# Attention in chunks with a mixture of experts behind it: x's transposes placed ahead of the expert's blocks, and the weight steps spread otherwise

## The chip, the cores and the metric

The kernel runs on one core of one Trainium2 chip, in one launch. The time is what the device takes for one execution, in microseconds. Each number of the trace comes from one profiled execution; the time before is the median of three others.

The engines: TensorE (PE; PEld is its weight load) multiplies matrices, VectorE (DVE), ScalarE (ACT) and GpSimd (POOL) do elementwise work, and SyncE (SP) issues most DMAs. Each engine takes its instructions in the order in which the program gives them.

## The reference, cut to what matters

Attention with a decaying state, over 4 batches, 8 heads, 768 positions and head dimension 48, then eight experts (3072 tokens, width 384, hidden width 1024) under a gate that is normalised eight times over both axes:

```python
def _attn_ref(r, k, v, w, u):
    for t in range(S):
        kt, vt, rt = (k[:, :, t], v[:, :, t], r[:, :, t])
        cur = np.einsum('bhd,bhe->bhde', u[None] * kt, vt)
        y[:, :, t] = np.einsum('bhd,bhde->bhe', rt, state + cur)
        state = w[None, :, :, None] * state + np.einsum('bhd,bhe->bhde', kt, vt)
    return y

def _moe_ref(x, w_gate, w1, w2):
    logits = x @ w_gate
    logits = logits - logits.max()
    P = np.exp(logits)
    for _ in range(8):
        P /= P.sum(1, keepdims=True) + 1e-09
        P /= P.sum(0, keepdims=True) + 1e-09
        P *= N / E
    for e in range(E):
        h = np.maximum(x @ w1[e], 0.0)
        ye = h @ w2[e]
        out += P[:, e:e + 1] * ye
    return out
```

The attention's output, with heads and head dimension joined, is x of the experts.

## The kernel before, in words

Attention runs in 24 chunks of 128 positions (`NTT` = 24, six for each batch). Inside a chunk the decay is folded into the operands: r is multiplied by a table `rtab`, k by `ktab` (which follow from w and are made once, at the start, by a scan, a reciprocal and some transposes), so that scores and state are plain matrix products. The large products of the experts are made in three parts from halves in 16 bit: each operand is split into a high half and the low rest.

One loop, lines 756 to 811, runs 27 rounds, i = 0 to 26 (this text counts rounds by i, so that round 4 is the fifth). In a round three chunks are in work at different stages. In the order of the code:

- `prep(i+2)` (L493): `rp` = r times `rtab` on GpSimd, `kp` = k times `ktab` on VectorE. `bonus_dot(i+1)` (L499): two products into `rk` on GpSimd. `stage_b(i+1)` (L518): the transposes of rp and kp on TensorE, and their copies rT and kT by ScalarE.
- `scale_x(i-2)` (L606): ScalarE scales x by a power of two into `xsc`.
- `work(1)` (L729): one block of expert 0. Up to round 4, where none is ready, `spin(3)` stands in its place, three matmuls on zeros into a tile of the PSUM pool `ps2`.
- `bonus(i)` (L508): VectorE sums `rk` to `dg`, and GpSimd makes two products from it, written over `rk`; a piece of `hbx` is the second input of the last. `stage_c(i)` (L529): the scores `pA`, which VectorE copies under a mask into `at`, then `pu`, which is added to the state `S` on VectorE and scaled on GpSimd.
- `work(1)` up to round 8, `work(2)` in rounds 9 to 24 (L781 and 782).
- `stage_e(i-2)` (L612): three transposes of `xsc` into `px`, a tile of `ps2`; ScalarE casts it to the high half of x (the CAST to `hbx`), VectorE subtracts this from `px` to get the low half (`hbx<-px,hbx`). In rounds 25 and 26 `work(2)` stands behind it.
- `prepare` (L725), as often as the first number of the round in `STEPS`: one step from the list `side`.
- `stage_d(i-1)` (L573): `py`, then x = py + bonus on VectorE, its maximum `xm`, the scale (`inv_s`, `xs`).
- `prepare`, as often as the second number, then `stage_f(i-3)` (L620): six gate matmuls into `px` from `wgp` and x of this round (a tile of x has its halves in `hbx`), and the logits (`lparts`) on VectorE.

The first 24 steps of `side` split expert 0's two weights, for each of them: three maxima (`wm`) over 1024 columns, the maximum over all partitions, the scale, then high halves (ScalarE, `ws<-ws,sw`) and low halves (VectorE, `ws<-ws,sw,ws`). Behind them come steps that rebuild x of three groups of tokens and make the sums of their quarters (17 sums on GpSimd for each group, `ws<-ws` on 256 columns, after three rebuilds on VectorE); a group's steps wait in the list until its tiles have been emitted.

A block is one of two units. `g1_unit` (L214): nine matmuls into `ph`, in the pool `ps1` (2 buffers), followed by a ScalarE activation to `hb` (high half) and a VectorE operation on `ph` and `hb` (low half). `g2_half` (L236), the half of a second product: 12 matmuls into `po`, which ScalarE copies to `stg` and a DMA takes to HBM. `po` has two buffers, which it shares with `px` and the tile of `spin`. Units that the loop leaves over run behind it, one for each step of the gate's normalisation (from L988). There are 64 first-product units and 48 halves of second products. The table and the places of the blocks are these:

```python
    STEPS = {
        0: (2, 2), 1: (0, 2), 2: (3, 1), 3: (1, 1),
        4: (1, 1), 5: (1, 1), 6: (2, 2), 7: (1, 1), 8: (1, 1),
    }
```

All operations are recorded by a helper, so that L29 is the line of nearly every row.

Of the kernel before, what the change touches and what calls it, by code (L numbers as in the profile page):

```python
# [32 lines left out]
def rwkv_sinkhorn_moe(  # L33
# [13 lines left out]
    V, S_, G, T, Q = (  # L47
        InOrder(tc, e) for e in (nc.vector, nc.scalar, nc.gpsimd, nc.tensor, nc.sync)
    )
# [8 lines left out]
    NTT = NT // P  # L58
# [5 lines left out]
    HP = 64  # L64
# [193 lines left out]
    def whole(gen):  # L258
        for _ in gen:
            pass  # L260

    def merged(g1, g2):
        for n in range(max(len(g1), len(g2))):
            yield from g1[n : n + 1]
            yield from g2[n : n + 1]
# [20 lines left out]
    def spin(n):  # L286
        pz = ps2.tile([P, TB], F32, tag="po", name="pz")
        for _ in range(n):
            T.matmul(pz, zeros[:, :P], zeros, start=True, stop=True)
# [13 lines left out]
    def load_chunk(tt):  # L303
        for nm, src in (("r", r), ("k", k), ("v", v)):
            load_part(tt, nm, src)
# [36 lines left out]
    def fill(x_):  # L342
        n = x_.shape[1]
        S_.mul(
            x_.rearrange("p (a q) -> p a q", q=HP),
            unit[:, :1, 1:].broadcast_to([P, n // HP, HP]), 0.0,
        )
# [16 lines left out]
    at_ = [ac.tile([P, H, C], F32, name=f"at{i}") for i in range(2)]  # L364

    ss_ = [ac.tile([P, NPAIR, 2, D], F32, name=f"S{i}") for i in range(3)]
    for t_ in rp_ + kp_:
        G.memset(t_[:, :, D:], 0.0)
    for t_ in ss_:
        for j in range(2):  # L370
            G.memset(t_[j * HP : (j + 1) * HP, :, 1 - j, :], 0.0)
    fill(at_[0].rearrange("p h c -> p (h c)"))

    rk0 = at2.tile([P, H, D], F32, tag="rk", name="rk_0", bufs=3)
    G.tensor_tensor(rk0, loads[0]["r"], loads[0]["k"], op=ALU.mult)
# [99 lines left out]
    def gate_max():  # L475
        V.tensor_reduce(wgm, wg, axis=AX.XY, op=ALU.max, apply_absolute_value=True)

    def gate_across():
        res = over_partitions(wgm, 1, ps1, "ph", "wg")
        next(res)  # L480
        return res

    def gate_split(res):
        pow2_scale(next(res), iswg, swg, 0.25)
        S_.activation(wgh, wg, AF.Copy, scale=swg)
        V.scalar_tensor_tensor(wgl, wg, swg, wgh, op0=ALU.mult, op1=ALU.subtract)
# [6 lines left out]
    def prep(tt):  # L493
        ld_ = loads[tt]
        G.tensor_tensor(rp_[tt % 2][:, :, :D], ld_["r"], rt4, op=ALU.mult)
        V.tensor_tensor(kp_[tt % 3][:, :, :D], ld_["k"], kt4, op=ALU.mult)
        st[tt] = {}

    def bonus_dot(tt):  # L499
        ld_ = loads[tt]  # L500
        rk = rk0
        if tt:
            rk = at2.tile([P, H, D], F32, tag="rk", name=f"rk_{tt}", bufs=3)
            G.tensor_tensor(rk, ld_["r"], ld_["k"], op=ALU.mult)
        G.tensor_tensor(rk, rk, ub, op=ALU.mult)
        st[tt]["rk"] = rk

    def bonus(tt):  # L508
        vn = loads[tt]["v"]
        dg = at2.tile([P, H], F32, tag="dg", name=f"dg_{tt}")  # L510
        V.tensor_reduce(dg, st[tt]["rk"], axis=AX.X, op=ALU.add)
        av = st[tt].pop("rk")
        G.tensor_tensor(av, vn, dg.unsqueeze(2).broadcast_to([P, H, D]), op=ALU.mult)
        aq = av.rearrange("p h d -> p (h d)").rearrange("p (a q) -> p a q", q=P // 2)
        G.tensor_tensor(aq, aq, xadd(tt), op=ALU.add)
        st[tt]["av"] = av

    def stage_b(tt):  # L518
        d = st[tt]
        for nm, src in (("rT", rp_[tt % 2]), ("kT", kp_[tt % 3])):  # L520
            pt = ps3.tile([P, NPAIR, P], F32, tag="pa", name=f"p{nm}_{tt}")
            sv = src.rearrange("p (a j) d -> p a (j d)", j=2)
            for p_ in range(NPAIR):
                T.transpose(pt[:, p_, :], sv[:, p_, :], ident)
            dst = at2.tile([P, NPAIR, P], F32, tag=nm, name=f"{nm}_{tt}", bufs=3 if nm == "rT" else 2)
            S_.copy(dst, pt)
            d[nm] = dst
# [78 lines left out]
    def scale_x(tt):  # L606
        d = st[tt]
        xs = at2.tile([P, DM], F32, tag="xsc", name=f"xsc_{tt}")
        S_.activation(xs, d["x"], AF.Copy, scale=d["s"])
        d["x"] = xs  # L610

    def stage_e(tt, bank_):  # L612
        d = st[tt]
        pt = bank_[:, :DM].rearrange("p (c q) -> p c q", q=P)
        for c in range(KC):
            T.transpose(pt[:, c, :], d["x"][:, c * P : (c + 1) * P], ident)
        S_.copy(xall(tt, 0), pt)
        V.tensor_tensor(xall(tt, 1), pt, xall(tt, 0), op=ALU.subtract)

    def stage_f(tt, bank_):  # L620
        pg = bank_[:, DM : DM + 2 * E]
        for c in range(KC):
            xh_, xl_ = xall(tt, 0)[:, c, :], xall(tt, 1)[:, c, :]

            T.matmul(
                pg, xh_, wgp[:, c].rearrange("p l e -> p (l e)"), start=(c == 0), stop=False,
                skip_group_check=True,
            )
            T.matmul(
                pg[:, :E], xl_, wgh[:, c, :], start=False, stop=(c == KC - 1), skip_group_check=True  # L630
            )
        V.tensor_scalar(
            lparts[:, tt].rearrange("p l e -> p (l e)"), pg, inv_s[:, tt : tt + 1], iswg,
            op0=ALU.mult, op1=ALU.mult,
        )
        del st[tt]
# [88 lines left out]
    def prepare():  # L725
        if side and need.get(id(side[0]), 0) <= emitted[0]:
            side.pop(0)()

    def work(n, ready=True):  # L729
        if not ready:  # L730
            spin(3)
            return
        for _ in range(n):
            if units:
                whole(units.pop(0))
# [3 lines left out]
    for sg in range(3):  # L739
# [3 lines left out]

    STEPS = {
        0: (2, 2), 1: (0, 2), 2: (3, 1), 3: (1, 1),
        4: (1, 1), 5: (1, 1), 6: (2, 2), 7: (1, 1), 8: (1, 1),
    }

    def n_steps(i):
        return STEPS.get(i, (2, 2) if i < 22 else (3, 2))  # L750

    prep(0)
    prep(1)
# [2 lines left out]
    for i in range(NTT + 3):  # L756
        if i == 1:
            gate_max()
        if i + 2 < NTT:
            if i + 4 < NTT:  # L760
                load_chunk(i + 4)
            if i == 0:
                Q.dma_start(raws[1], w2[0].rearrange("(c p) d -> p c d", p=P))
            prep(i + 2)
        if i + 1 < NTT:
            bonus_dot(i + 1)
        if i + 1 < NTT and i:
            stage_b(i + 1)
        if 2 <= i <= NTT + 1:
            scale_x(i - 2)  # L770
        work(1, i > 4)
        if i < NTT:
            bonus(i)
            if ("S", i) in st:
                st[i]["S"] = st.pop(("S", i))
            stage_c(i)
        if i == 2:
            gate_split(gate_res)
        if i == 0:
            stage_b(1)  # L780
        if i <= NTT:  # L781
            work(2 if i > 8 else 1, i > 4)
        if i == 1:
            gate_res = gate_across()
        if i >= 2:
            bank_ = ps2.tile([P, TB], F32, tag="po", name=f"px_{i}")
        if 2 <= i <= NTT + 1:
            stage_e(i - 2, bank_)
            emitted[0] = i - 1
        if i > NTT:  # L790
            work(2)
        for _ in range(n_steps(i)[0]):
            prepare()
        if 1 <= i <= NTT:
            stage_d(i - 1)
        for _ in range(n_steps(i)[1]):
            prepare()
        if 3 <= i:
            stage_f(i - 3, bank_)
        done = i - 2  # L800
        if 0 <= done < NTT and done % TH == TH - 1:
            po_ = done // TH
            if po_ == 0:
                units += [g1_unit(0, fc, W) for fc in range(FC)]
                units += [g2_half(0, t, 0, W) for t in range(TH)]
                pend = [(0, t, 1) for t in range(TH)]
            for j in range(2 if po_ else 0):
                g1 = [g1_unit(po_, fc, W) for fc in range(j * FHC, (j + 1) * FHC)]
                g2 = [g2_half(*a, W) for a in pend]
                units += merged(g1, g2)  # L810
                pend = [(po_, t, j) for t in range(TH)]
# [401 lines left out]
    for s in range(NS):  # L1213
        tasks = stage_tasks(s)
        for g in range(NG):
            for j in range(2):
                for n, nxt in enumerate(g1_slots(s, g, j)):
# [3 lines left out]
                    i = j * NPR + n  # L1221
# [37 lines left out]
```

## Time and profile before

| | |
|---|---|
| time, median of 3 runs (lowest, highest) | 1546.42 us (1546.19, 1547.11) |
| profiled execution | 1546.49 us |
| its span | 1544.80 us |
| mean granted clock of TensorE, share of full speed | 0.999 |
| busy: TensorE, VectorE, ScalarE, GpSimd | 1524.8, 1021.6, 673.3, 590.3 us |
| read from and written to HBM | 55.39 and 80.23 MB |

The span runs from the first instruction to the last; the profiled execution's time has 1.69 us around it. A row of the trace gives an engine, the operation, the tile that it writes and the tiles that it reads (output <- inputs), the partitions and elements, and how many instructions of the kind follow one another. `[1.66 <-DVE hbx L29]` says that the engine stood idle for 1.66 us before, and that the last thing it waited for was VectorE's write of `hbx`.

### The profile page before, as it was taken

How to read it: one execution, taken by the hardware profiler on the slowest of the kernel's cores; microseconds unless marked ns; L12 is line 12 of the kernel's file. 1: busy time of each engine (PE TensorE's matmuls, PEld its weight loads, DVE VectorE, ACT ScalarE, POOL GpSimd, SP SyncE). 2: the span in 40 equal slices, each digit the busy share in tenths (PEclk: the TensorE clock that was granted, in tenths of full speed). 3: DMA queues.
4: the chain of work that ended last, by engine and by line, in shares of the span. 5: the costliest groups of instructions: out<-in, count | busy, mean ns of one | idle time of the engine just before them, and what ended most of it. 6: DMA issues, size and time to landing. Idle time of an engine off the chain costs nothing.

```text
span 1544.8 us, 26300 instructions
## 1 busy us (share of the span) xinstructions
PE 1524.8 (99%) x10385; PEld 865.9 (56%) x10385; DVE 1021.6 (66%) x1714; ACT 673.3 (44%) x1192; POOL 590.3 (38%) x708
## 2 busy tenths in 40 slices
PE   8899999999999999999999999999999999999999
PEld 5677776655555555555555555555555555555555
DVE  8977776866666666666666666656566666666554
ACT  4334334434444454545444444535354444535320
POOL 8778874320202424242433424242423324242200
PEclk9999999999999999999999999999999999999999
DMA  8343413121225566576667666655545555556433
GB/s 193 77 90 89 100 33 99 50 72 55 93 59 105 78 125 90 84 122 85 125 89 129 84 121 88 123 68 96 57 61 94 61 96 60 98 58 99 53 95 130
DMA packets 167647, 138.40 MB, mean 90 GB/s; under 512 B 90337, under 2 KB 161762, under 8 KB 167522
## 3 DMA queue, kind: packets, MB, share of 16 engines
q0 software_dynamic: 44928, 61.36, 32.9%
q1 hardware_dynamic: 122384, 75.35, 17.5%
q8 instruction: 81, 1.33, 0.4%
q14 instruction: 44, 0.36, 0.1%
q10 hardware_dynamic: 210, 0.00, 0.0%
HBM read 55.39 MB, written 80.23 MB: 88 GB/s over the span
## 4 chain that ended last, share of the span: by engine, by line
PE 90%; DVE 4%; POOL 3%; issue 1%; ACT 1%; DMA 0%; POOLq 0%; ACTq 0%; DVEq 0%
PE po L29 47%; PE bZ L29 12%; PE bY L29 12%; PE bA L29 5%; PE bB L29 5%; PE ph L29 4%; PE bC L29 2%; POOL rk L29 2%; PE py L29 1%; PE pA L29 1%; DVE ws L29 0%; PE px L29 0%; POOL ws L29 0%; POOL rp L29 0%; DVE hbx L29 0%
## 5 line engine op out<-in xcount | busy, mean ns | idle before, releaser
L29 PE MATMUL po<-ws,hbx 128*128 128x384 f16 x3360 | 737.2, 326 | 0.0
L29 POOL DMA_DIRECT2D accd<-stg x288 | 249.7, 867 | 695.0 <-ACT stg L29 672.6
L29 PEld LDWEIGHTS <-hbx 128*128 128x128 f16 x3504 | 334.5, 98 | 299.9 <-issue 7.0
L29 PEld LDWEIGHTS <-ws 128*128 128x128 f16 x3096 | 301.3, 98 | 244.9 <-issue 2.0
L29 ACT ACTIVATE hbx<-tb 128x512 f16<-128x512 f32 x224 | 141.0, 629 | 450.2 <-DVE tb L29 450.2
L29 PE MATMUL po<-ws,hb 128*128 128x384 f16 x1248 | 323.2, 326 | 0.0
L29 DVE TENSOR_TENSOR tb<-bY,tb 128x512 f32<-128x512 f32 x168 | 116.2, 692 | 195.8 <-PE bY L29 195.6
L29 ACT ACTIVATE stg<-po,pe 128x384 f32<-128x384 f32 x312 | 179.1, 574 | 122.1 <-PE po L29 96.5
L29 PE MATMUL bZ<-xv,ws 128*128 128x512 f16 x840 | 227.1, 379 | 0.5 <-DVE tb L29 0.4
L29 PE MATMUL bY<-xv,ws 128*128 128x512 f16 x840 | 227.1, 379 | 0.0
L29 DVE TENSOR_TENSOR tb<-bZ,tb 128x512 f32<-128x512 f32 x168 | 115.6, 688 | 136.1 <-PE bZ L29 136.1
L29 PEld LDWEIGHTS <-hb 128*128 128x128 f16 x1248 | 121.3, 98 | 93.5 <-issue 0.3
L29 POOL TENSOR_TENSOR ucb<-rawb 128x256 f32<-128x256 f32 x84 | 75.7, 951 | 118.7 <-DVE tb L29 79.0
L29 DVE TENSOR_TENSOR tb<-bB,tb 128x512 f32<-128x512 f32 x112 | 77.5, 692 | 49.2 <-PE bB L29 47.3
L29 PE MATMUL ph<-hbx,ws 128*128 128x384 f16 x576 | 104.4, 327 | 0.5 <-DVE hb L29 0.5
L29 DVE SCALAR_TENSOR_TENSOR hb<-tb,hbx 128x512 f16<-128x512 f32 x112 | 77.3, 690 | 24.6 <-ACT hbx L29 19.4
L29 PE MATMUL bB<-xv,ws 128*128 128x512 f16 x336 | 90.8, 379 | 0.0
L29 PE MATMUL bA<-xv,ws 128*128 128x512 f16 x336 | 90.8, 379 | 0.0
L29 DVE SCALAR_TENSOR_TENSOR hbx<-tb,hbx 128x512 f16<-128x512 f32 x112 | 77.5, 692 | 14.7 <-ACT hbx L29 10.4
L29 ACT COPY tb<-bZ 128x512 f32<-128x512 f32 x56 | 32.8, 585 | 65.5 <-PE bZ L29 65.5
L29 DVE SCALAR_TENSOR_TENSOR hb<-ph,hb 128x384 f16<-128x384 f32 x64 | 35.5, 554 | 37.5 <-ACT hb L29 37.1
L29 ACT ACTIVATE hb<-ph 128x384 f16<-128x384 f32 x64 | 31.1, 487 | 57.9 <-PE ph L29 57.5
(169 smaller groups left out, 1550.1 us busy)
## 6 DMA issues: line engine op xcount, KB each, us to landing
accd<-stg POOLq DMA_DIRECT2D x288, 192.0 KB, 3.7
rawb<-in_moe_w_dram SPq DMA_DIRECT2D x28, 768.0 KB, 6.7
e0d<-stg SPq DMA_DIRECT2D x48, 192.0 KB, 2.0
hb<-e0d SPq DMA_DIRECT2D x48, 192.0 KB, 3.8
vn<-in_v_dram SPq DMA_DIRECT2D x24, 192.0 KB, 2.8
accd<-stg SPq DMA_DIRECT2D x24, 192.0 KB, 1.8
accd<-hb POOLq DMA_DIRECT2D x24, 192.0 KB, 4.8
rawb<-accd SPq DMA_DIRECT2D x24, 192.0 KB, 2.4
```

The lines of the kernel that those rows point to most:

```text
L29: return lambda *a, **k: self.tc.keep_in_program_order(f(*a, **k))
```

## The change

Three things are changed.

1. At the start six memsets of the state tiles `S` on GpSimd go; in their place ScalarE fills each of the three tiles whole, with `fill` (a multiplication by 0.0), behind the fill of the first `at` tile, which now comes ahead of them.
2. In the loop the second call of `work` stands behind `stage_e` in all rounds, not in 25 and 26 alone. It is left out in rounds 8 and 9; from round 10 on it is for two blocks. So rounds 8 and 9 have one block each, not two and three.
3. In `STEPS` round 4 has no step, and what stood from round 4 to round 8 is done one round later. The five steps for each round begin with round 20, not 22.

```diff
--- before.py
+++ after.py
@@ -366,10 +366,9 @@
     ss_ = [ac.tile([P, NPAIR, 2, D], F32, name=f"S{i}") for i in range(3)]
     for t_ in rp_ + kp_:
         G.memset(t_[:, :, D:], 0.0)
+    fill(at_[0].rearrange("p h c -> p (h c)"))
     for t_ in ss_:
-        for j in range(2):
-            G.memset(t_[j * HP : (j + 1) * HP, :, 1 - j, :], 0.0)
-    fill(at_[0].rearrange("p h c -> p (h c)"))
+        fill(t_.rearrange("p a j d -> p (a j d)"))
 
     rk0 = at2.tile([P, H, D], F32, tag="rk", name="rk_0", bufs=3)
     G.tensor_tensor(rk0, loads[0]["r"], loads[0]["k"], op=ALU.mult)
@@ -743,11 +742,11 @@
 
     STEPS = {
         0: (2, 2), 1: (0, 2), 2: (3, 1), 3: (1, 1),
-        4: (1, 1), 5: (1, 1), 6: (2, 2), 7: (1, 1), 8: (1, 1),
+        4: (0, 0), 5: (1, 1), 6: (1, 1), 7: (2, 2), 8: (1, 1), 9: (1, 1),
     }
 
     def n_steps(i):
-        return STEPS.get(i, (2, 2) if i < 22 else (3, 2))
+        return STEPS.get(i, (2, 2) if i < 20 else (3, 2))
 
     prep(0)
     prep(1)
@@ -778,8 +777,6 @@
             gate_split(gate_res)
         if i == 0:
             stage_b(1)
-        if i <= NTT:
-            work(2 if i > 8 else 1, i > 4)
         if i == 1:
             gate_res = gate_across()
         if i >= 2:
@@ -787,8 +784,8 @@
         if 2 <= i <= NTT + 1:
             stage_e(i - 2, bank_)
             emitted[0] = i - 1
-        if i > NTT:
-            work(2)
+        if i not in (8, 9):
+            work(2 if i > 9 else 1, i > 4)
         for _ in range(n_steps(i)[0]):
             prepare()
         if 1 <= i <= NTT:
```

The order of the instructions on three engines, at three places, before and after the change. The number at the end of a name is a running number of the tile; the one before it is the chunk or round.

VectorE in round 4, before: from the low half of x (`hbx`, round 4's `px`) to round 5's `kp`.

```order
L29 TENSOR_TENSOR hbx_72<-px_4_839,hbx_72 128x3x128
L29 TENSOR_REDUCE wm_0_319<-ws0_74 128x1
L29 TENSOR_TENSOR x_3_871<-py_3_846,rk_3_530 128x384
L29 TENSOR_REDUCE xm_3_873<-x_3_871 128x1
L29 TENSOR_SCALAR inv_s_83<-xm_3_873 128x1
L29 TENSOR_SCALAR inv_s_83<-inv_s_83 128x1
L29 RECIPROCAL xs_3_875<-inv_s_83 128x1
L29 TENSOR_REDUCE wm_0_319<-ws0_74 128x1
L29 TENSOR_SCALAR lparts_82<-px_4_839,inv_s_83,iswg_313 128x16
L29 TENSOR_TENSOR kp1_169<-kn_7_648,ktab_285 128x8x48
```

And the same place after the change.

```order
L29 TENSOR_TENSOR hbx_72<-px_4_832,hbx_72 128x3x128
L29 TENSOR_TENSOR x_3_867<-py_3_842,rk_3_527 128x384
L29 TENSOR_REDUCE xm_3_869<-x_3_867 128x1
L29 TENSOR_SCALAR inv_s_83<-xm_3_869 128x1
L29 TENSOR_SCALAR inv_s_83<-inv_s_83 128x1
L29 RECIPROCAL xs_3_871<-inv_s_83 128x1
L29 TENSOR_SCALAR lparts_82<-px_4_832,inv_s_83,iswg_310 128x16
L29 TENSOR_TENSOR kp1_169<-kn_7_645,ktab_282 128x8x48
```

The two maxima of the weights (`wm`) have left the round; one comes back behind the low half in round 5, and the rest follow in their turn.

ScalarE in rounds 8 and 9, before: `hb<-ph` and `stg<-po` are the copies of expert 0's blocks, the CAST is x's high half.

```order
L29 ACTIVATE xsc_6_1306<-x_6_1264,xs_6_1268 128x384
L29 ACTIVATE hb3_73<-ph_0_6_1308 128x384
L29 ACTIVATE hb3_73<-ph_0_7_1357 128x384
L29 CAST hbx_72<-px_8_1369 128x3x128
L29 ACTIVATE ws1_75<-ws0_74,sw_0_318 128x1024
L29 COPY rT_10_1434<-prT_10_1429 128x512
L29 COPY kT_10_1441<-pkT_10_1436 128x512
L29 ACTIVATE xsc_7_1443<-x_7_1402,xs_7_1406 128x384
L29 COPY stg0_0_0_1458<-po_0_0_1445 128x384
L29 COPY stg0_1_0_1511<-po_1_0_1498 128x384
L29 COPY stg0_2_0_1527<-po_2_0_1514 128x384
L29 CAST hbx_72<-px_9_1530 128x3x128
```

And after the change.

```order
L29 ACTIVATE xsc_6_1300<-x_6_1256,xs_6_1260 128x384
L29 ACTIVATE hb3_73<-ph_0_6_1302 128x384
L29 CAST hbx_72<-px_8_1351 128x3x128
L29 ACTIVATE ws1_75<-ws0_74,sw_0_315 128x1024 x2
L29 COPY rT_10_1416<-prT_10_1411 128x512
L29 COPY kT_10_1423<-pkT_10_1418 128x512
L29 ACTIVATE xsc_7_1425<-x_7_1383,xs_7_1387 128x384
L29 ACTIVATE hb3_73<-ph_0_7_1427 128x384
L29 CAST hbx_72<-px_9_1476 128x3x128
```

In round 8 one first-product block is left, and its partner has become the only block of round 9; the three copies of second-product blocks have left these rounds.

TensorE in round 24, before: the last matmuls of the round's third block, x's transposes, and the first matmuls of `py`.

```order
L29 MATMUL ph_4_1_3696<-hbx_72,ws1_75 128x384
L29 LDWEIGHTS ws1_75
L29 MATMUL ph_4_1_3696<-hbx_72,ws1_75 128x384
L29 MATMUL px_24_3708<-ident_84,xsc_22_3666 128x128 x3
L29 MATMUL py_23_3717<-S1_174,rT_23_3406 64x96 x8
```

And after the change.

```order
L29 MATMUL ph_3_6_3623<-hbx_72,ws1_75 128x384
L29 LDWEIGHTS ws1_75
L29 MATMUL ph_3_6_3623<-hbx_72,ws1_75 128x384
L29 MATMUL px_24_3635<-ident_84,xsc_22_3621 128x128 x3
L29 LDWEIGHTS hb3_73
```

The transposes now stand behind the round's first block; a second-product block follows them, where the rows end, and one more block comes ahead of `py`.

## Rows read from the trace of the kernel before

**Rows 1.** Busy time of each engine, with its share of the span.

```profile
PE 1524.8 (99%) x10385; PEld 865.9 (56%) x10385; DVE 1021.6 (66%) x1714; ACT 673.3 (44%) x1192; POOL 590.3 (38%) x708
```

**Rows 2.** Waits of TensorE, 30 to 92.5 us: total us, times, longest.

```profile
PE px L29 <- DVE hbx L29: 4.7, 5, 1.7
```

**Rows 3.** Waits of TensorE, 92.5 to 262 us.

```profile
PE px L29 <- DVE hbx L29: 2.5, 4, 1.3
```

**Rows 4.** Stretch 34 to 92.5 us: busy by engine, clock, DMA share, GB/s.

```profile
34.00:92.50 58.50, 50.34 (x811) 38.20 (x811) 55.02 (x114) 24.76 (x43) 44.08 (x45) 1.00 0.43 84
```

**Rows 5.** Timeline of the start: start us, duration us, engine, operation.

```profile
7.78 1.25 POOL L29 TENSOR_TENSOR rk<-rn,kn 128x384 f32<-128x384 f32 x1
8.15 0.90 DVE L29 TENSOR_TENSOR good<-wt,wsafe 128x4 f32<-128x4 f32 x1
8.27 0.41 ACT L29 COPY hb<-hb 128x256 f32<-128x256 f32 x1 [1.39 <-DVE hb L29]
...
11.27 0.15 DVE L29 TENSOR_TENSOR wc<-hb 128x4 f32<-128x4 f32 x1
...
12.90 1.01 POOL L29 TENSOR_TENSOR rp<-rn,rtab 128x384 f32<-128x384 f32 x1 [3.87 <-ACT rtab L29]
```

**Rows 6.** Timeline of VectorE, rounds 4 to 7.

```profile
51.22 1.21 DVE L29 TENSOR_REDUCE wm<-ws 128x1 f32<-128x1024 f32 x1
...
62.78 1.24 DVE L29 TENSOR_TENSOR kp<-kn,ktab 128x384 f32<-128x384 f32 x1
...
66.83 0.56 DVE L29 SCALAR_TENSOR_TENSOR hb<-ph,hb 128x384 f16<-128x384 f32 x1
67.31 0.55 DVE L29 TENSOR_TENSOR hbx<-px,hbx 128x384 f16<-128x384 f32 x1
...
76.06 0.56 DVE L29 TENSOR_TENSOR x<-py,rk 128x384 f32<-128x384 f32 x1
...
77.69 1.54 DVE L29 SCALAR_TENSOR_TENSOR ws<-ws,sw,ws 128x1024 f16<-128x1024 f32 x1
```

**Rows 7.** Timeline of GpSimd, the bonus of round 5.

```profile
56.84 0.83 POOL L29 TENSOR_TENSOR rk<-vn,dg 128x384 f32<-128x384 f32 x1 [1.70 <-DVE dg L29]
57.75 1.00 POOL L29 TENSOR_TENSOR rk<-rk,hbx 128x384 f32<-128x384 f32 x1
```

**Rows 8.** Timeline of TensorE: gate matmuls of rounds 4, 5, 9, 10, round 5's first block.

```profile
51.36 0.29 PE L29 MATMUL px<-wgp,hbx 128*128 128x16 f16 x6 [1.66 <-DVE hbx L29]
...
52.41 1.63 PE L29 MATMUL ph<-hbx,ws 128*128 128x384 f16 x9
...
59.91 0.29 PE L29 MATMUL px<-wgp,hbx 128*128 128x16 f16 x6 [1.21 <-DVE hbx L29]
...
95.38 0.31 PE L29 MATMUL px<-wgp,hbx 128*128 128x16 f16 x6
...
105.23 0.30 PE L29 MATMUL px<-wgp,hbx 128*128 128x16 f16 x6
```

**Rows 9.** Chain that ended last, in time order: start us, us, piece.

```profile
69.88 1.46 PE ph L29 x9
...
72.37 0.60 PE pu L29 x16
...
85.80 1.95 PE po L29 x12
```

**Rows 10.** Timeline of GpSimd, rounds 9 and 10: first token sum, state behind the bonus.

```profile
99.27 1.09 POOL L29 TENSOR_TENSOR ws<-ws 128x256 f32<-128x256 f32 x1 [5.71 <-DVE ws L29]
...
105.18 1.26 POOL L29 TENSOR_TENSOR S<-S,wbd 64x192 f32<-64x192 f32 x2
```

**Rows 11.** Timeline, rounds 23 to 25: gate matmuls, xsc, transposes.

```profile
233.78 0.31 PE L29 MATMUL px<-wgp,hbx 128*128 128x16 f16 x6
...
235.71 0.62 ACT L29 ACTIVATE xsc<-x,xs 128x384 f32<-128x384 f32 x1 [3.02 <-DVE xs L29]
...
243.57 0.55 PE L29 MATMUL px<-ident,xsc 128*128 128x128 f32 x3 [0.32 <-ACT xsc L29]
```

## The prediction, made before the changed kernel was run

> **What bounds the kernel now.** I read the busy shares first: TensorE is busy for 1524.8 of 1544.8 us [rows 1], so a change of order can give back no more than its 20 us of idle time. The waits of TensorE by stretch come next. From 30 to 92.5 us it waits 4.7 us in five places for the low half of x (px <- DVE hbx) [rows 2], from 92.5 to 262 us 2.5 us in four places for the same thing [rows 3]; the edit can touch little else. The windows show why the first stretch is slow: of the 58.5 us from 34 to 92.5 us VectorE is busy for 55.0, TensorE for 50.3, with the granted clock at 1.00, the 2.4 GHz level [rows 4]. There VectorE's queue sets the time, and a block of expert 0 taken out of that stretch shortens nothing: its matmuls come back later at full price. From round 9 on TensorE is the bound again.
>
> The profiled execution took 1546.49 us (span 1544.80, 1.69 around it); the median of the runs is 1546.42. I work differences against the span and add them to the median.
>
> **Start.** Six memsets of the S tiles leave GpSimd, which afterwards waits 3.87 us for rtab anyhow: the removal itself gives nothing. ScalarE gets three fills of 384 columns. Its copy at 8.27 us had waited 1.39 us [rows 5]; by that copy's 0.41 us for 256 columns a fill takes at most 0.62, three 1.86. Half a microsecond late is hidden by VectorE's reciprocal, for whose result the same readers wait: nothing. Without this cover it would be the 0.5. But rk, GpSimd's first product, follows the other memsets at once. Before, it ran from 7.78 to 9.03 us, and VectorE's compare `good` on 4 columns, issued at 8.15, ended with it: 0.90 us, where wc, of the same size, takes 0.15 [rows 5]. All that leads to rtab hangs on it. If rk is over by then, 0.75 us is won; if its loads land no sooner, or it now holds up the operations ahead of `good`, nothing, and a loss is excluded only by the 3.87 us that GpSimd has to spare. I take a gain of 0.3, nearer to nothing, as these operations stand closest.
> The Trainium skill (SBUF — State Buffer, Who interferes with whom) says that a VectorE instruction with two SBUF inputs contends with a GpSimd instruction that reads SBUF, not with one that only writes. By it the memsets blocked nobody, and rk in their place can block the scan ahead of `good`: the gain would be 0 and not 0.3, and the sum 0.3 higher. The trace agrees for `good`; for the scan no row before shows it.
>
> **Rounds 0 to 3.** Earlier transposes change nothing: the low half's place on VectorE is the same, as no block runs yet and VectorE has no gap.
>
> **Rounds 4 to 10, on VectorE's queue.** The edit takes two weight maxima out of round 4, each 1.21 us, of which 0.08 lies under the next (the overlap seen between hb at 66.83 and hbx at 67.31) [rows 6]: 1.13 net. The prices that I use, start to start: x with its scale 1.63 (76.06 to 77.69), a block's low part hb or the low half hbx 0.48, logits 0.20, one low step of the weights 1.46; kp to the end of S is 4.05 with kp stretched to 1.24 (62.78 to 67.31 without one hb) and 3.36 with kp as short as hbx, an operation of the same width (0.55) [rows 6].
> Round 4: the gate matmuls stay at 51.36 [rows 8], since the low half precedes the first maximum. x starts at 51.22 and not 52.35; logits end at 53.05, 2.25 us sooner than before.
> Round 5: TensorE now leads. Its first block starts at 52.41, takes 1.46 [rows 8, 9] and ends at 53.9, the ScalarE copy of it at 54.45, hb and the dot dg behind it at 55.5. GpSimd's two bonus steps take 1.91, and from their end to the gate matmuls 1.16 pass (58.75 to 59.91) [rows 7, 8]. So the gate comes at 58.6, not 59.91: 1.3 gained. But VectorE stands idle for a good microsecond at the low half, which now has nothing ahead of it. Then hb, one maximum, x, the other maximum and logits: 63.0 us, where before kp started at 62.78 with one maximum more behind it. The lead is spent.
> Rounds 6 to 9, one after the other on VectorE, with kp taken as stretched in rounds 7 and 8 only: round 6 kp to S 3.36, then hbx, hb, maximum, x, logits and a small reduce, 70.35. Round 7: S ends at 74.4, hbx, hb, then the two small steps of the weights' maximum (0.5), for which the gate waits (about 76), x, scale and logits: 78.1. Round 8 (one block): the dot ends at 80.3, the bonus at 82.2, hbx follows the cast and ends at 83.2, x and one low step: 86.5. Round 9: 3.36 and hbx: gate at 90.5. Before it stood at 95.38 with three second-product blocks more, 1.95 each [rows 8, 9]; without them 89.5. So here the change is 1.0 us late: VectorE was the bound, and the blocks had been covering it.
> Round 10: two second-product blocks stand behind the transposes, and these hold one of the two PSUM buffers, so the second block waits until the first is copied out: the copy's 0.48 and its start, 0.55. Together +1.5 us. If kp is stretched in all four rounds it is 1.4 more, if in none 1.4 less.
> The second half of the weights is later by a round, but the first second-product block, in round 10, comes after the low step that it needs, about level with it.
>
> **Rounds 11 to 25.** The 2.5 us of waits [rows 3] fall away in rounds 13 and 19, where the low half is now long done. In rounds 11 and 17 (i mod 3 = 2: the cast of x then overwrites the group of three tiles that the bonus reads) it still waits for GpSimd. The token sums start one round later there: GpSimd's first sum waits for the last of three rebuilds, which I put 2.6 us behind the gate (x 1.63, a rebuild of 768 columns at twice the 0.48 of 384). From that sum to the end of the bonus took 5.9 us (99.27 to 105.18) [rows 10], the way to the gate 1.16: 9.7. TensorE's round without pu is 9.25 (105.23 less 95.38, less pu's 0.60) [rows 8, 9]: 0.4 is left in each, 0.8 together. Rounds 14 and 20 I put at nothing, as the bonus ended well before the gate one round earlier; if GpSimd is as late there, 0.4 each.
> New is a wait in rounds 24 and 25. Round 24 has no scores, so x's transposes now stand behind one block, done 1.8 us after the gate of round 23 at 233.78; xsc ends at 236.33 [rows 11], so 0.8. In round 25 the wait of 0.32 is there already, behind a second-product block; the block that stands there now is a first-product one, 0.49 shorter: 0.5 more. Sum: -2.5 + 0.8 + 1.3 = -0.4.
>
> **Tail.** Three more blocks run beside the gate's iterations: their price is in the 89.5 above. TensorE is full there; I take 0 (between -0.5 and +0.5).
>
> Sum: -0.3 + 1.5 - 0.4 + 0 = +0.8 us: **1547.2 us**. A measurement of this kernel tells 0.2%, 3.1 us, from no change; this is well within.
>
> **Rivals.**
> *The lead of round 4 lasts (faster).* If the low half no longer waits anywhere and VectorE's idle time is not lost to the bonus, the three waits of rounds 5, 7 and 8 (1.8 of the 4.7 us; the rest lies in rounds 3 and 4, ahead of the edit, 1.66 of it in the row of 51.36) and the 2.5 us go, the start gives 0.7 and no new wait comes: 5 us, 1541.4 [rows 2, 3, 8]. For it: low halves are done before the blocks in two rounds out of three. Against: VectorE is busy 94% of that stretch, and its work there shrinks by 2.6 us while TensorE's shrinks by 5.9. Chance 0.15.
> *ScalarE and VectorE stand behind GpSimd (slower).* In every third round the cast of x now stands ahead of the block's copies on ScalarE and hbx ahead of hb on VectorE, so both wait until the bonus is done. It decides where the bonus ends less than 1.16 us before the gate. Were the first sum as late behind the gate as it was (99.27 less 95.38, 3.9) [rows 8, 10], the way would be 11.0 and the wait 1.7, in rounds 11, 14, 17 and 20: 6.8 in place of the 0.8 counted, and x's scale late for the next transposes. Sum 6.8 us, 1553.2. For it: GpSimd has no gap in these rounds. Against: the rebuilds are now two ahead of x. Chance 0.15; if it holds in half of the rounds, 1550.
> *The change does no more than move waits (forecast).* 0.70; alone it lies between 1544.5 and 1549.5: kp's 1.4 either way, the start's 0.3 and 0.45, rounds 14 and 20, the tail.
>
> Range 1543.0 to 1550.8: it leaves out most of the first rival and the far end of the second. Faster by over 0.2% (below 1543.3): 0.15 and a little of the forecast, 0.17; slower (above 1549.5): 0.18; within: 0.65.
>
> **What would show it.** Right: TensorE's wait for hbx near 0 in rounds 13 and 19, gate matmuls of round 5 near 58.6 and of round 9 near 90.5 us, waits for hbx in rounds 8 and 9 of about 1 us, a new wait po <- ACT stg of 0.5 in round 10, px <- ACT xsc of 0.8 in each of rounds 24 and 25, three blocks more behind the last gate matmuls. Wrong: a gate of round 9 at 89 or earlier, waits of 1.5 us in rounds 11, 14, 17 and 20, or rtab more than 0.7 us earlier.

## The result: 0.26% slower, and the profile after

| | before | after |
|---|---|---|
| median of ten runs (lowest, highest) | 1546.38 us (1546.19, 1547.11) | 1550.99 us (1549.09, 1551.60) |
| profiled execution | 1546.49 us | 1550.92 us |
| its span | 1544.8 us | 1549.2 us |
| mean granted clock | 0.999 | 0.997 |

The ratio is 1.0026 (95% interval 1.0017 to 1.0034). The forecast was +0.8 us and "no change"; the change costs 4 to 4.6 us. By the ratio it is at 1550.4, inside the range but near its end; the median itself lies 0.2 us above that end.

The runs of the changed kernel spread more than those of before, 2.5 us against 0.9, and not evenly: three lie at 1549.1 to 1549.3, six at 1550.9 to 1551.6. That is part of the explanation below.

The waits of TensorE in the changed kernel, from 30 to 92.5 us (total us, times, longest):

```profile
PE px L29 <- DVE hbx L29: 2.7, 3, 1.5
PE pmax_w L29 <- DVE md_w L29: 1.5, 1, 1.5
```

The 4.7 us of before [rows 2] have become 2.7, but a wait for the maximum of the weights has grown to 1.5. Before, in the same stretch, it was

```profile
PE pmax_w L29 <- DVE md_w L29: 0.4, 1, 0.4
```

And after the change, from 92.5 to 262 us:

```profile
PE px L29 <- DVE hbx L29: 2.7, 3, 1.4
PE px L29 <- ACT xsc L29: 1.6, 2, 0.8
PE po L29 <- ACT stg L29: 0.6, 1, 0.6
```

There the 2.5 us of before [rows 3] are 2.7, 1.4 of it the wait of round 9, whose gate matmuls had none before and came behind 92.5 us. The wait for a block's copy (`stg`) is new; that for `xsc` was 0.3 us, once [rows 11].

The windows of the same profile show what I had not foreseen (us, busy time and count of PE, PEld, DVE, ACT and POOL, granted clock, DMA share, GB/s):

```profile
34.00:92.50 58.50, 50.87 (x829) 39.02 (x830) 52.27 (x113) 24.53 (x42) 42.53 (x45) 0.94 0.43 83
...
38.00:42.00 4.00, 3.67 (x33) 2.43 (x32) 3.94 (x8) 1.87 (x3) 2.89 (x5) 0.57 0.69 129
...
74.00:76.00 2.00, 0.53 (x11) 0.40 (x7) 1.93 (x6) 0.00 (x0) 1.85 (x4) 0.98 0.32 65
76.00:79.40 3.40, 3.40 (x20) 2.55 (x21) 2.73 (x10) 1.69 (x3) 2.44 (x3) 0.51 0.30 61
79.40:82.00 2.60, 2.60 (x55) 1.93 (x54) 1.23 (x3) 0.49 (x1) 0.13 (x1) 1.00 0.55 107
```

In this stretch the granted clock was 1.00 before [rows 4]. Now it falls twice to half, the 1.2 GHz level: near 38 us and, behind two microseconds in which TensorE was busy for 0.53, from 76.0 to 79.4 us.

The gate matmuls of rounds 5 and 8 to 10, and the second-product block of round 10 that waits, on TensorE's timeline after the change:

```profile
58.32 0.29 PE L29 MATMUL px<-wgp,hbx 128*128 128x16 f16 x6
...
84.94 0.29 PE L29 MATMUL px<-wgp,hbx 128*128 128x16 f16 x6 [0.89 <-DVE hbx L29]
...
92.88 0.29 PE L29 MATMUL px<-wgp,hbx 128*128 128x16 f16 x6 [1.42 <-DVE hbx L29]
...
100.68 2.11 PE L29 MATMUL po<-ws,hb 128*128 128x384 f16 x12 [0.57 <-ACT stg L29]
...
104.45 0.30 PE L29 MATMUL px<-wgp,hbx 128*128 128x16 f16 x6
```

Round 5 comes 1.6 us earlier than before and round 9 2.5 us earlier [rows 8]; but three blocks, 5.85 us of work, are missing ahead of round 9.

So the useful measure is **lateness**: the time of a round's gate matmuls, less the time that they had before, plus the price of the blocks that are still outstanding (1.46 us for a first product, 1.95 for half a second one [rows 9]). For round 9 it is 92.88 - 95.38 + 5.85 = 3.35 us. I use it for every run below.

### The profile page after: what moved, and what is told of

It is laid out like the page before. It is cut to its first block, busy times and chain, and to the rows that moved or that the text cites. A ratio compares the mean times of both kernels' runs of the same rounds, so it can differ in the third digit from the quotient of the medians.

```text
span 1549.2 us, 26293 instructions
## 1 busy us (share of the span) xinstructions
PE 1528.9 (99%) x10385; PEld 867.6 (56%) x10385; DVE 1023.7 (66%) x1714; ACT 675.9 (44%) x1195; POOL 589.2 (38%) x702
## 4 chain that ended last, share of the span: by engine, by line
PE 90%; DVE 5%; POOL 2%; issue 0%; ACT 0%; DMA 0%; SPq 0%; POOLq 0%; DVEq 0%; ACTq 0%
PE po L29 47%; PE bZ L29 12%; PE bY L29 12%; PE bA L29 5%; PE bB L29 5%; PE ph L29 4%; PE bC L29 2%; PE py L29 1%; POOL rk L29 1%; PE pA L29 1%; PE px L29 1%; DVE ws L29 0%; DVE hb L29 0%; PE pu L29 0%; PE prT L29 0%
## 5 line engine op out<-in xcount | busy, mean ns | idle before, releaser
L29 DVE TENSOR_REDUCE wms<-rawb 128x1 f32<-128x768 f32 x56 | 51.8, 944 | 0.0
```

The costliest lines, as they stand in the source:

```text
L29: return lambda *a, **k: self.tc.keep_in_program_order(f(*a, **k))
```

## The experiments

### The parts of the change, one by one

Each kernel is the one before with one part of the change; the last has two. The weight steps were not run by themselves.

**The start alone.**

```diff
+    fill(at_[0].rearrange("p h c -> p (h c)"))
     for t_ in ss_:
-        for j in range(2):
-            G.memset(t_[j * HP : (j + 1) * HP, :, 1 - j, :], 0.0)
-    fill(at_[0].rearrange("p h c -> p (h c)"))
+        fill(t_.rearrange("p a j d -> p (a j d)"))
```

> The kernel before with the start of the change alone: three fills on ScalarE in place of six memsets on GpSimd. Theory 1 (the loss of 4.6 us lies in rounds 8 to 10, where VectorE's queue sets the time and blocks were taken out, and in rounds 24 and 25): nothing but the start moves, 0 to -0.3 us, 1546.1 to 1546.4. Theory 2 (the loss begins at the start: round 3's gate matmuls came 0.45 us later in the changed kernel, behind a stretch at half clock): half a microsecond to 2 us slower, 1547 to 1548.5, with the half-clock stretch at 38 us there in this run too.

Measured: 1546.15 us against 1546.73, ratio 0.9997 (0.9988 to 1.0006). Its profile has a half-clock stretch near 38 us as well and lost nothing by it: its gate matmuls come 0.27 us early in round 4 and 0.23 early in round 26. Theory 2 is out. On its timeline of the start (start us, duration):

```profile
5.93 1.00 POOL L29 TENSOR_TENSOR rk<-rn,kn 128x384 f32<-128x384 f32 x1
...
7.52 0.70 DVE L29 TENSOR_TENSOR_SCAN hb<-hb 128x260 f32<-128x260 f32 x1
...
8.13 0.14 DVE L29 TENSOR_TENSOR good<-wt,wsafe 128x4 f32<-128x4 f32 x1
...
10.55 0.16 DVE L29 TENSOR_TENSOR wc<-hb 128x4 f32<-128x4 f32 x1
```

`good` takes 0.14 us with rk out of its way, 0.90 before [rows 5], and `wc` starts 0.72 us earlier; two thirds of that are gone by round 4. How much is left there differs from profile to profile: in the seven profiles here with the fills the start of round 3's kp lies between 0.84 us ahead of before and 0.14 behind it, and in the five other runs, without the fills, between 0.19 ahead and 0.56 behind. So one profile does not tell a gain of 0.27 from none.

**The transposes alone.**

```diff
-        if i <= NTT:
-            work(2 if i > 8 else 1, i > 4)
 ...
-        if i > NTT:
-            work(2)
+        work(2 if i > 8 else 1, i > 4)
```

> The kernel before with the second call of work behind the transposes in every round, the number of blocks and the steps as before. Theory 1: the waits for the low half in rounds 11 to 23 fall (2.5 us before), rounds 24 and 25 lose 1.5, round 9, where two second-product blocks now stand behind the transposes, loses the 0.6 that round 10 lost in the changed kernel: about -0.5 to +0.5, 1546 to 1547. Theory 3 (the transposes are the loss, as the copies of the blocks now stand behind the cast and the low half): 3 us or more slower, 1549.5.

Measured: 1546.83 us, ratio 1.0002 (0.9993 to 1.0011). Theory 3 is out. The lateness changes by +1.0 in round 9 (0.6 expected), -0.8 in round 11, -1.2 in round 17 and +1.0 in round 24; at the end it is +0.5.

**The blocks alone**: one in rounds 8 and 9, in place of two and three.

```diff
-        if i <= NTT:
-            work(2 if i > 8 else 1, i > 4)
+        if i <= NTT and i not in (8, 9):
+            work(2 if i > 9 else 1, i > 4)
```

> The kernel before with one block in rounds 8 and 9 in place of two and three, nothing else: the first weight steps stand where they stood. Theory 1: VectorE's queue holds the gate matmuls of rounds 8 and 9, the three blocks come back behind the loop at 5.85 us and the rounds get shorter by half of that at most: 2 to 3.5 us slower, 1548.5 to 1550, and TensorE waits for the low half in rounds 8 and 9 for 1 us each or more. Theory 4 (the blocks cost nothing, the weight steps that moved a round later are the loss): within 0.5 us of before, with both rounds shorter by what the blocks took.

Measured: 1551.28 us, ratio 1.0029 (1.0018 to 1.0041): the whole loss and a little more, and 1.3 us over the most that I expected by theory 1. Theory 4 is out. Its timeline of TensorE, rounds 8 and 9 and the first operations of round 10:

```profile
84.75 0.29 PE L29 MATMUL px<-wgp,hbx 128*128 128x16 f16 x6 [1.88 <-DVE hbx L29]
...
93.50 0.30 PE L29 MATMUL px<-wgp,hbx 128*128 128x16 f16 x6 [2.23 <-DVE hbx L29]
93.66 1.09 PE L29 MATMUL prT<-ident,rp 128*128 128x128 f32 x4
94.55 1.06 PE L29 MATMUL pkT<-ident,kp 128*128 128x128 f32 x4
95.40 2.90 PE L29 MATMUL po<-ws,hb 128*128 128x384 f16 x12
```

Round 8 comes at 84.75 us where it came at 84.58 with one block more: the block's 1.46 us have become a wait. Behind the wait of 2.23 us the transposes take 1.09 and 1.06 us, in place of 0.64 and 0.60 elsewhere: here too the clock falls behind the longest wait (0.57 granted from 93 to 97 us). Lateness rises by 1.6 us up to round 10; round 11, which has no wait for the low half here, makes up 0.85 of it.

**The blocks and the weight steps**: the same, and in `STEPS`

```diff
-        4: (1, 1), 5: (1, 1), 6: (2, 2), 7: (1, 1), 8: (1, 1),
+        4: (0, 0), 5: (1, 1), 6: (1, 1), 7: (2, 2), 8: (1, 1), 9: (1, 1),
 ...
-        return STEPS.get(i, (2, 2) if i < 22 else (3, 2))
+        return STEPS.get(i, (2, 2) if i < 20 else (3, 2))
```

> The one before with the weight steps a round later as well (no step in round 4, five for each round from round 20): the changed kernel without the start and without the transposes. Theory 1: as the run with the blocks alone or up to 1 us slower, 1549 to 1551, since the steps only move within VectorE's full queue. Theory 4: 3 to 4.5 us slower than that run. Theory 3: about 1 us over before or less, since the transposes stand as before.

Measured: 1550.67 us, ratio 1.0023 (1.0013 to 1.0032), like the blocks alone. In its profile round 9's gate comes at 91.02 us, 2.5 us before that of the last run (2.1 of it behind round 4), as the steps relieve VectorE's queue ahead of it; but rounds 11 and 17 wait 1.7 us each for the low half, and a half-clock stretch behind round 17's gate costs another 1.7.

### How the loss depends on the block that is taken out

**One block in round 8, three in round 9.**

```diff
-        if i <= NTT:
+        if i <= NTT and i != 8:
```

> The kernel before with one block in round 8 in place of two; round 9 keeps three. Theory 1 (a block taken out of a round that VectorE sets shortens nothing): round 8's gate matmuls stay near 84.6, TensorE waits there about 1.9 us in place of 0.46, and the block is paid behind the loop: 1.3 to 2 us slower, 1548 to 1548.5. Theory 8 (each block taken out costs its share of the loss whichever round it leaves): 4.5 us for three, 1.5 for one here and 1.5 in the next run as well.

**Two in round 8, two in round 9.**

```diff
-            work(2 if i > 8 else 1, i > 4)
+            work(2 if i > 9 else 1, i > 4)
```

> The kernel before with two blocks in round 9 in place of three; round 8 keeps two. Theory 1: TensorE sets round 9 before the change, and VectorE is ready at about 93.5 us (that is where the gate stood in the run with one block), so the gate matmuls come at 93.4 to 93.6 in place of 95.38, the round gets shorter by nearly the whole block (1.95), and the time stays: 0 to 0.5 us slower, 1546.7 to 1547.2. Theory 8: 1.5 us slower.

Measured: 1549.43 us, ratio 1.0020 (1.0011 to 1.0029), and 1548.23, ratio 1.0010 (1.0001 to 1.0019), against 1546.53. The first block costs more than was expected, the second much more: by the times alone theory 8, with 1.5 us for each, does better on the second run than theory 1. The gate matmuls of rounds 8 and 9 in the one and in the other:

```profile
85.17 0.29 PE L29 MATMUL px<-wgp,hbx 128*128 128x16 f16 x6 [1.89 <-DVE hbx L29]
95.49 0.31 PE L29 MATMUL px<-wgp,hbx 128*128 128x16 f16 x6
```

```profile
84.80 0.29 PE L29 MATMUL px<-wgp,hbx 128*128 128x16 f16 x6 [0.46 <-DVE hbx L29]
93.66 0.31 PE L29 MATMUL px<-wgp,hbx 128*128 128x16 f16 x6
```

In the loop theory 1 holds. With one block in round 8 the lateness rises by 1.48 us in that round, and the wait is 1.89 us. With two in round 9 the gate comes 1.72 us earlier, without a wait, and round 9's lateness is 0.23 like that of round 8: this block is free there. At the end of the loop the lateness is 2.05 and 0.60, of which 0.56 and 0.21 were there in round 4 already, ahead of the edits. But the spans are 3.0 and 1.6 us over before: in both, about 1 us more is lost behind the loop. The rows of the second run there:

```profile
276.91 0.27 PE L29 MATMUL pmax_s<-ident,wmas 128*2 128x128 f32 x1 [0.78 <-DVE wmas L29]
...
279.30 0.34 PE L29 MATMUL po<-ws,hb 128*128 128x384 f16 x1 [0.33 <-DVE hb L29]
```

One block left over in place of none or three puts other units beside the steps of the gate's normalisation, and two waits of 1.1 us in all appear. A wait of 0.5 that the kernel before has there falls away, so the waits explain 0.6 of the 1 us. The changed kernel, with three left over, has none of the three; its tail gives 0.4 back (4.83 late at the end of the loop, span 4.4 longer). I had expected a price of blocks alone, and not that their number decides what stands beside what.

### The clock

**The changed kernel with its idle time filled.**

```diff
             stage_d(i - 1)
+        if 7 <= i <= 9:
+            spin(4)
```

> The changed kernel with four matmuls on zeros behind py in rounds 7, 8 and 9, where TensorE stood idle for 1.47, 0.89 and 1.42 us: no work of the kernel moves, the idle time is filled. Theory 5 (part of the loss is TensorE's clock, which fell to half behind the idle time of round 7: the matmuls from 76.1 to 79.4 us took 1.6 us longer): no half-clock stretch behind rounds 7 to 9, round 9's gate matmuls near 91.3 and not 92.88, and 1549.0 to 1549.6 us in the median. Theory 6 (VectorE sets these rounds, the clock is only a sign of it): round 9's gate matmuls stay at 92.9, time 1551.

Measured: 1549.98 us, ratio to before 1.0022 (1.0013 to 1.0031). The clock stays up in rounds 7 to 9 of its profile: from the gate of round 7 to that of round 8 pass 7.42 us, in the changed kernel 9.02, and from there to round 9 7.94 in both. Round 9 comes at 91.84 us and not near 91.3, as round 4 was already 0.6 later. That is theory 5 in the profile. The median, above the 1549.0 to 1549.6 expected, does not settle it: it is 1 us under the first measurement of the changed kernel, no better than the second (below), and the highest of the 11 runs is 1551.84. The filler is not free either. Its tile takes one of the two buffers of `po`, and in round 10 x's transposes wait 0.26 us for the logits (`lparts`), which they do in neither profile of the changed kernel: from the gate of round 9 to that of round 10 pass 11.88 us and not 11.57.

**The changed kernel once more, and with two rounds in the old order.** The second kernel leaves rounds 8 and 9 as they are:

```diff
+        if i in (10, NTT):
+            work(2)
 ...
-        if i not in (8, 9):
+        if i not in (8, 9, 10, NTT):
```

> The changed kernel once more, as it is, beside the next two on the same chip. Theory 5 (the clock takes part of the loss): the time depends on whether the half-clock stretch falls into rounds 7 to 10: where this profile has none there, its execution is near 1549.2 us and round 9's gate matmuls come near 91.3; where it has one, near 1551 and 92.9. Theory 6: the same gate times either way.

> The changed kernel with the blocks of rounds 10 and 24 ahead of the transposes again, as they stood before the change; the rest of it stays. Theory 1: the wait of 0.6 us for a block's copy in round 10 and that of 0.8 for xsc in round 24 fall away: 1.2 to 1.8 us faster than the changed kernel beside it. Theory 7 (what is won in the loop is given back behind it): no more than 0.4 us.

Measured: 1549.94 us, ratio 1.0024 (1.0013 to 1.0034), and 1548.48, ratio 1.0018 (1.0009 to 1.0027), against 1546.34. The medians are 1.5 us apart, as expected of theory 1; but the clock may have a part in that, as it fell in one of the two profiles and not in the other (below). From round 9 on, behind the fall, the lateness rises by 1.46 us in the one and 0.69 in the other, so the profiles give the order 0.8 us: 0.8 won in round 10, 1.0 in round 24, and 1.0 lost in round 11, whose gate matmuls then wait longer for the low half. In the changed kernel and with the order restored:

```profile
113.83 0.29 PE L29 MATMUL px<-wgp,hbx 128*128 128x16 f16 x6 [0.61 <-DVE hbx L29]
```

```profile
112.66 0.29 PE L29 MATMUL px<-wgp,hbx 128*128 128x16 f16 x6 [1.63 <-DVE hbx L29]
```

Theory 7 falls: behind the loop both give back 0.3 to 0.4 us.

These two profiles decide about the clock, because up to round 9 the kernels are the same. The changed kernel has a half-clock stretch from round 7 to 8; its gate matmuls of rounds 7 to 9, the block between, and the window:

```profile
75.59 0.30 PE L29 MATMUL px<-wgp,hbx 128*128 128x16 f16 x6
...
76.66 2.96 PE L29 MATMUL ph<-hbx,ws 128*128 128x384 f16 x9
...
84.35 0.29 PE L29 MATMUL px<-wgp,hbx 128*128 128x16 f16 x6 [0.60 <-DVE hbx L29]
```

```profile
76.50:80.00 3.50, 3.50 (x20) 1.76 (x22) 2.00 (x7) 1.85 (x4) 1.61 (x2) 0.54 0.55 106
```

Its round 9 comes at 92.30 us, its execution took 1550.30. The other one has no such stretch:

```profile
75.51 0.30 PE L29 MATMUL px<-wgp,hbx 128*128 128x16 f16 x6
...
76.59 1.63 PE L29 MATMUL ph<-hbx,ws 128*128 128x384 f16 x9
...
82.94 0.29 PE L29 MATMUL px<-wgp,hbx 128*128 128x16 f16 x6 [0.88 <-DVE hbx L29]
...
90.87 0.29 PE L29 MATMUL px<-wgp,hbx 128*128 128x16 f16 x6 [1.41 <-DVE hbx L29]
```

```profile
76.50:80.00 3.50, 3.50 (x62) 2.49 (x61) 3.14 (x10) 1.93 (x4) 1.66 (x3) 1.00 0.57 110
```

Round 7 is 0.08 us apart, round 8 1.41 and round 9 1.43: the fall costs 1.35 us and nothing of it is made up, since hb, and with it VectorE's queue, waits for the block: 1.58 us with the fall, 0.25 without. Theory 6 is out. The stretches near 38 us, by contrast, cost nothing that is left at round 4, and VectorE was busy for 3.94 of the 4 us there. The changed kernel's first profile has one and its second has none, and round 4 comes 0.32 us later in the first; but so does round 3's kp, which starts ahead of the stretch:

```profile
37.56 1.35 DVE L29 TENSOR_TENSOR kp<-kn,ktab 128x384 f32<-128x384 f32 x1
```

```profile
37.24 1.36 DVE L29 TENSOR_TENSOR kp<-kn,ktab 128x384 f32<-128x384 f32 x1
```

**Both**: the order of the second kernel and the filler of the first.

> The one before with four matmuls on zeros in rounds 7 to 9 as well. Theories 1 and 5 together: what the run with the filler and the run with the order each win adds up, 1548 to 1548.6 us, and what is left over before, about 2 us, is the three blocks that came out of rounds 8 and 9 (the two blocks there, taken out one at a time, cost 2.9 and 1.7). Theory 8: nothing more than the order's share.

Measured: 1548.56 us, ratio 1.0017 (1.0008 to 1.0026). Beside the order alone the filler gives nothing in the median, as theory 8 said; in round 10 a block waits 0.16 us for the logits, as with the filler above. Its runs lie closer (eight of eleven between 1548.0 and 1549.2; without it six between 1547.8 and 1548.5 and five between 1549.7 and 1550.9). The 2 us left over before are, as expected, of the size of the lateness at the end of the loop, 2.40. So the clock's price is shown by the gate times of two profiles; that it is part of the medians is argued and not shown, as the filler betters neither the median of the order alone nor that of the changed kernel's second measurement.

### A version that is faster than both

The blocks and steps of before, the fills at the start, and the transposes ahead only where the waits were:

```diff
-        if i <= NTT:
+        if i <= NTT and not 10 <= i < NTT:
             work(2 if i > 8 else 1, i > 4)
 ...
-        if i > NTT:
+        if i > NTT or 10 <= i < NTT:
             work(2)
```

> The kernel before with the fills at the start, and with the transposes ahead of the second call of work in rounds 10 to 23 alone; blocks and steps as before. Theory 1: the waits for the low half in rounds 11, 13, 17 and 19 fall away (2.5 us before, 2.1 of it won in the run with the transposes alone), round 9 loses no wait for a copy, rounds 24 and 25 nothing, the start gives 0.2: 1.5 to 2.3 us faster than before, 1544.3 to 1545.1. Theory 7 (what the transposes win is given back behind the loop): within 0.5 us of before.

Measured: 1544.94 us, ratio 0.9990 (0.9981 to 0.9999): 1.6 us faster than before, as expected, with an interval that just excludes no change. TensorE's waits from 92.5 to 262 us:

```profile
PE px L29 <- DVE hbx L29: 0.8, 1, 0.8
PE px L29 <- ACT xsc L29: 0.3, 1, 0.3
```

Of four waits for the low half one is left, in round 11, where I had expected none. The kernel's lateness falls from 0.2 to -1.0 between rounds 9 and 24, and the span follows it. The fills give nothing in this profile, which is 0.12 us late in round 4.

## Why the prediction was right or wrong

Lateness in us, as predicted and as three profiles have it (the last differs from the change in rounds 10 and 24, so it has no entry from there on):

| | predicted | changed | changed, again | order restored |
|---|---|---|---|---|
| round 4 | -0.3 | -0.45 | -0.77 | -0.86 |
| round 9 | +0.7 | +3.35 | +2.77 | +1.34 |
| round 10 | +1.2 | +4.09 | +3.51 | |
| round 23 | -0.5 | +3.31 | +2.72 | |
| rounds 25, 26 | +0.8 | +4.83 | +4.24 | |
| span | +0.8 | +4.4 | +3.8 | |

That the time by the ratio, 1550.4 us, lies inside the range is luck as far as the mechanism goes: the upper part of the range was there for the second rival, and the loss came by another way. The sum's +0.8 us is a fifth of it.

**What held.** The mechanism of rounds 4 to 9: VectorE's queue sets them, the lead of round 5 (58.6 us forecast, 58.32 measured) is spent by round 7, and a block taken out of there "shortens nothing: its matmuls come back later at full price". The runs with one block less show it for round 8. Forecast and found too: round 7 at about 76 (75.92), a wait of 0.5 for the copy in round 10 (0.57), waits of 0.8 for xsc in rounds 24 and 25 (0.81 each), no wait for the low half in rounds 13 and 19, three blocks behind the loop. In the start, rk ran ahead of `good` and got out of its way: `wc` started 0.72 us earlier, of which 0.27 were left by round 4 in the run with the start alone. That this is near the 0.3 that I took is in part luck, as round 4's lateness in the table runs from -0.45 to -0.86. By the Trainium skill (SBUF — State Buffer, Who interferes with whom) a VectorE instruction with two SBUF inputs contends with a GpSimd one that reads SBUF. The rows agree with the page for `good`, 0.90 us beside rk and 0.14 without it. They do not bear out what I drew from it, that rk would block the scan and the gain be 0: rk was over at 6.93 us and the scan began at 7.52.

**What failed**, by the steps of the sum:

- *The granted clock was taken as 1.00 throughout.* The step "Round 9: 3.36 and hbx: gate at 90.5" had no term for a fall. With TensorE at full clock round 9 came at 90.87; with the fall at 92.30 and 92.88. That is 1.35 us of the error in the second profile and 1.6 in the first (9.02 us from round 7 to 8, not 7.43). I had read the wait in round 7 ("the two small steps of the weights' maximum (0.5), for which the gate waits") and did not ask what 1.5 us of idle time do to the clock behind it.
- *kp in round 9, and the bonus of round 8.* I took kp as stretched in rounds 7 and 8 only; in round 9 it takes 1.15 us, not 0.55. The rows of the run with the order restored, kp of rounds 8 and 9 and the low half between:

```profile
77.32 1.19 DVE L29 TENSOR_TENSOR kp<-kn,ktab 128x384 f32<-128x384 f32 x1
...
82.33 0.56 DVE L29 TENSOR_TENSOR hbx<-px,hbx 128x384 f16<-128x384 f32 x1 [0.65 <-ACT hbx L29]
...
86.23 1.15 DVE L29 TENSOR_TENSOR kp<-kn,ktab 128x384 f32<-128x384 f32 x1
```

  This 0.6 is one round's share of the bound "in all four rounds it is 1.4 more". From round 4's gate to that of round 9 I had forecast 39.1 us (51.36 to 90.5), and 40.4 passed (50.50 to 90.87). Of the 1.2 that the sum lacks, kp is half; another 0.5 arose in round 8, where from the start of kp to the end of the low half 5.57 us passed and not 5.1 (78.1 to 83.2). The table shows only half of it, as round 4 came 0.56 us earlier than forecast.
- *Rounds 11 to 23: -1.7 forecast, -0.8 measured.* The token sums begin 2.86 us behind round 10's gate, not 2.6; the rows of the changed kernel:

```profile
107.31 1.09 POOL L29 TENSOR_TENSOR ws<-ws 128x256 f32<-128x256 f32 x1 [4.19 <-DVE ws L29]
...
112.27 1.00 POOL L29 TENSOR_TENSOR rk<-rk,hbx 128x384 f32<-128x384 f32 x1
```

  From that sum to the bonus's end are 5.96 us, and the gate follows 1.16 later, as forecast; so rounds 11 and 17 still wait 0.62 and 0.61 and not 0.4. The rest is 0.04 to 0.07 in each round without a wait, for which I had no term. It lies in the block that now stands right ahead of `py`: in round 21 of the run with the transposes alone, from the start of the last two blocks to the next matmuls pass 3.02 us, and 2.93 in the same round before. The transposes themselves, from their start to the next, take 0.38 us where they now stand and 0.42 where they stood.
- *Tail.* 0 forecast, -0.4 measured, within what was allowed.

Together for the second profile: 0.8 + 1.35 (clock) + 1.0 (up to round 10 without it) + 0.9 (rounds 11 to 23) + 0.2 (rounds 24 and 25) - 0.4 (tail) = 3.85, where its span is 3.8 longer.

**The rivals.** The faster one fell in round 7 (its 1.8 us of waits are 1.9 by the rows: 1.21, 0.24 and 0.46). The slower one, ScalarE and VectorE standing behind GpSimd, exists at 0.6 us in rounds 11 and 17 and not at all in 14 and 20; the kernel became slower by another way. That the change does no more than move waits, at 0.70, was the wrong case: two waits, in rounds 7 and 8 to 9, became lost work and a lower clock.

**What stays open**: why the clock falls behind round 7 in some executions and not in others. The idle time ahead of it was 1.47 us in the profiles with and without the fall. The times of the runs without a profile agree with one fall more or less (for the kernel with the order restored, 1547.8 to 1548.5 us at a mean clock of 0.999 or more, 1549.7 to 1550.9 at 0.998 or less), but their traces were not taken, and in the changed kernel's own runs the split is not as clean: its slowest, 1551.60 us, has a mean clock of 0.999. Whether VectorE's queue could be relieved in round 9, so that one block there is enough, was not tried.

## What to carry to other kernels

Work that fills TensorE's idle time is free where it stands and costs its full price where it goes: before blocks are moved out of a round, ask which engine sets that round, and count each block's price once where it leaves and once where it lands. Where TensorE gets a longer idle time, cost the work behind it at the lower clock too, as a case with a chance, for rows of another order do not show it. A change of several parts deserves a run for each: here one part by itself brought the whole loss, one was neutral with a winning half, and that half, with the fills, beat the kernel before by 1.6 us.

## What the runs showed of the hardware that I had not expected

- A VectorE operation on four columns took 0.90 us beside a GpSimd product of 384 columns, and 0.14 without it.
- Half-clock stretches come at different places in executions of one kernel, behind 1.5 us of idle time in one execution and not in another. One behind round 7 costs 1.35 us, as VectorE's queue waits for the slowed block; one near 38 us, where VectorE was busy for 3.94 of 4 us, costs nothing that is left at round 4.
- Three f32 transposes take 0.49 us behind a block of expert 0 and 0.55 behind `pu`, yet the next matmuls start 0.42 and 0.38 us after them: the length of the row is not its price.
